# Window attention and a feed-forward block in float32: from three split products to one plain product, on one Trainium2 core

## The chip, the cores and the metric

The kernel runs on one core of one Trainium2 chip. The metric is the device time of one execution in microseconds (us). A core has a matrix engine (TensorE: PE for its matrix multiplications, PEld for the loads of the stationary operand), a vector engine (DVE), an activation engine (ACT), GpSimd (POOL) and a queue that issues DMA transfers (SP). Each of them works through its own list of instructions in order; semaphores make one wait for another.

## The reference, cut to what matters

Attention over 8 batches and 8 heads: 512 local positions with a window of 32 to either side, 32 global positions, 64 features a head. Its output, one row of 512 features for every position, is the input of a feed-forward block with 2048 hidden features.

```python
k_all = np.concatenate([k_g, k_l], axis=2); v_all = np.concatenate([v_g, v_l], axis=2)
out_g = np.matmul(sm(scale * np.matmul(q_g, k_all.transpose(0, 1, 3, 2))), v_all)
s_ll = np.where(mask, scale * np.matmul(q_l, k_l.transpose(0, 1, 3, 2)), -1000000000.0)
s_lg = scale * np.matmul(q_l, k_g.transpose(0, 1, 3, 2))
out_l = np.matmul(sm(np.concatenate([s_lg, s_ll], axis=-1)), v_all)
x = concatenate([out_g, out_l], axis=2)      # to (8*544, 512)
h = x @ w_in                                 # 512 -> 2048
return (h - np.tanh(h)) @ w_out              # 2048 -> 512
```

The attention inputs are float32; the two weights arrive in a 64-bit format and are turned into float32 on the chip.

## The kernel before, in words

**The work.** All matrix products run on TensorE, into eight PSUM banks of 128 x 512 float32. There are two kinds of operand: plain float32 (`F32`) and the rounded type `F32R`. Where a product has `F32R` operands, each operand x is held as a high part (x rounded to `F32R`) and a low part (x minus the high part), and the product is the sum of three: high x high, high x low and low x high.

**Feed-forward** (class `Chunk`). One chunk is 512 rows (the 512 local positions of a batch) or, at the end, the 256 global rows of all batches. It has 16 steps (8 for the 256 rows), one for each 128 hidden features. In a step `add_hidden` issues three groups of four products of 128 x 128 by 128 x 512 (line 1054: high weights by high x, high weights by low x, low weights by high x), ACT takes the tanh (line 1062), DVE subtracts (line 1065), a copy rounds the result to `ghi` (line 1068) and POOL or DVE subtracts to get `glo` (line 1071). `add_out` issues three groups of four products (line 1102: `w_out_hi` by `ghi`, `w_out_lo` by `ghi`, `w_out_hi` by `glo`), which add up in four banks over all 16 steps. After the last step the four banks are copied out and stored (lines 1125 and 1130).

**Attention.** Batches 0 and 1 (class `Pair`, and `Head` with `plain`) work in plain float32, two heads together: keys and queries are turned by TensorE (line 479), the scores of the global queries are two products a pair (lines 512 and 513), the local scores four a head (line 766), the softmax is on DVE, ACT and POOL, the probabilities are turned by TensorE (lines 552 and 858), and eight products a head with the values follow (line 956). Batches 2 to 7 (class `Head`) work one head at a time with split operands: keys and queries are turned by DVE and split, DMA transfers put the parts one under the other, so that one product of 128 rows holds two of the three (lines 712, 713, 769, 770); the values and the probabilities are split too (line 956), and the turning of the next head's probabilities is put between the products (line 958).

**Weights.** `add_weights` loads each weight in 64 pieces of 128 x 256 (256 KB as they arrive), joins the two 32-bit words (lines 375, 379, 383) and splits the result into `w_in_hi`, `w_in_lo`, `w_out_hi`, `w_out_lo` (lines 386 and 389). The pieces are spread over batches 0 and 1.

**What sets the order.** No engine's order is written out. Class `Order` is a planner: every operation is added with the engines it may run on, a planned duration, a due time, what it reads and writes and the PSUM banks it takes. `run` places them one by one at the earliest start, ties going to the earlier due time, and the instructions are issued in that order. Due times come from a table of numbers (`CFG`). The feed-forward of batch b is placed among the attention of batch b + 1, so TensorE's list alternates between the two; batch 0's attention has no feed-forward beside it, and the last batch's feed-forward and the global rows have no attention beside them.

Of the kernel before, what the change touches and what calls it, by code (L numbers as in the profile page):

```python
# [9 lines left out]
F32R = mybir.dt.float32r  # L10
# [11 lines left out]


def f32(ap):
    return ap.bitcast(F32)
# [7 lines left out]
class Later:  # L33


    def __init__(self, pool, shape, tag):
        self.make = lambda: pool.tile(shape, F32R, name=tag, tag=tag)
        self.tile = None

    def __call__(self):  # L40
        if self.tile is None:
            self.tile = self.make()
        return self.tile


class Op:
    __slots__ = ("eng", "fn", "due", "n", "ready", "succ", "alloc", "free", "lat", "start", "end", "args", "seq", "xfer", "rows", "ldw", "tail", "lock")


class Order:  # L50
# [14 lines left out]
    def add(self, eng, fn, due, r=(), w=(), res=(), alloc=(), free=(), lat=0.0, xfer=0.0, rows=1.0, ldw=0.107, tail=0.107, lock=False):  # L65
# [5 lines left out]
        o.xfer, o.rows, o.ldw, o.tail = xfer, rows, ldw, tail  # L71
# [22 lines left out]

    def tensor_time(self, t, d, rows):
        t0 = t
        while d > 1e-9:
            i = int(t / self.TICK + 1e-9)
            rate = 1.0 if self.columns.get(i - 1, 0) >= 3060 else 0.5
            x = min(d / rate, (i + 1) * self.TICK - t)  # L100
            self.columns[i] = self.columns.get(i, 0) + x * rate * 2400 * rows
            d -= x * rate
            t += x
        return t - t0

    def run(self):
# [3 lines left out]
        tail = 0.0  # L110
# [5 lines left out]
        while left:  # L116
            best = None
            for o in ready:
# [13 lines left out]
                for e, (d, pen) in o.eng.items():  # L132
# [3 lines left out]
                    if e == "T":  # L136
                        s = max(s, at.get(e, 0.0) + self.XW * max(0.0, o.ldw - tail))
# [9 lines left out]
            if e == "T":  # L147
                s = max(at.get(e, 0.0) + max(0.0, o.ldw - tail), ready_at)
                d = self.tensor_time(s, d, o.rows)
                tail = o.tail  # L150
# [31 lines left out]
def kernel(ctx, tc, q_l, k_l, v_l, q_g, k_g, v_g, w_in, w_out, out):  # L182
# [7 lines left out]
    NF = DFF // P  # L190
    WIDE = w_in.dtype != F32
# [4 lines left out]

    NPG = 4 * P + 96
    pg = cp.tile([P, NPG], F32, name="pg")
    idr = cp.tile([P, P], F32R, name="idr")
    idn = f32(idr)  # L200
    masks = [cp.tile([P, KC], BF16, name=f"mask{j}") for j in range(3)]
    tile_mask = [masks[0]] + [masks[1]] * (NT - 2) + [masks[2]]


    rawkq = cp.tile([P, 2 * S], F32, name="rawkq")
    raw1, kq = rawkq[:, :S], rawkq[:, S:]
    wraw = [cp.tile([P, 256, 2], F32, name=f"wraw{j}") for j in range(3)]
    tt_ = [cp.tile([P, 512], F32, name=f"t{j}") for j in range(2)]
    gg = [[cp.tile([P, 512], F32R, name=f"g{n}{j}") for n in ("hi", "lo")] for j in range(2)]
    stats = [cp.tile([P, 16], F32, name=f"st{j}") for j in range(3)]  # L210
    gt = cp.tile([P, 5, G], F32, name="gt")
    qgt = cp.tile([P, H, 2, G], F32R, name="qgt")


    prob = [cp.tile([P, 2 * KC + G], F32, name=f"prob{j}") for j in range(2)]
    prob = [prob[t // 2][:, t % 2 * KC:t % 2 * KC + 256] for t in range(NT)]
    prob2 = [t.rearrange("p (a c) -> p a c", a=2)[:, j] for t in tt_ for j in range(2)]
    vraw = cp.tile([P, 2, NT, D], F32, name="vraw")

    w_in_hi = cp.tile([P, NCC, DFF], F32R, name="w_in_hi")  # L220
    w_in_lo = cp.tile([P, NCC, DFF], F32R, name="w_in_lo")
    w_out_hi = cp.tile([P, NF, DM], F32R, name="w_out_hi")
    w_out_lo = cp.tile([P, NF - 4, DM], F32R, name="w_out_lo")
    xg = cp.tile([P, NCC, B * G], F32, name="xg")

    first_raw = cp.tile([P, 2, 2, NT, 2, D], F32, name="first_raw", tag="x_hi1")  # L230
    first_raw = [first_raw[:, 0], first_raw[:, 1], rawkq.rearrange("p (a t h d) -> p a t h d", a=2, t=NT, h=2)]
    first_kw = cp.tile([P, 2, 2 * S], F32, name="first_kw", tag="x_lo1")
    first_kw = [first_kw[:, 0, :NT * KC], first_kw[:, 1, :NT * KC], cp.tile([P, NT * KC], F32, name="first_kw2", tag="kw")]
    first_kw = [x.rearrange("p (t c) -> p t c", t=NT) for x in first_kw]
    first_q = cp.tile([P, 4 * DM], F32, name="first_q", tag="w_out_lo4")
    first_q = [first_q[:, :S], first_q[:, S:2 * S], cp.tile([P, S], F32, name="first_q2", tag="hi0")]
    first_q = [x.rearrange("p (t c) -> p t c", t=NT) for x in first_q]
    first_m = cp.tile([P, 2 * S], F32, name="first_m", tag="hl")
    first_mask = first_m[:, :608]
    first_t = cp.tile([P, 2, 2, 320], F32, name="first_t0", tag="thi"), cp.tile([P, 2, 2, 320], F32, name="first_t1", tag="tlo")  # L240
    first_v = cp.tile([P, 2, NT, 2, D], F32, name="first_v", tag="vv")
    first_g = cp.tile([P, H // 2, G], F32, name="first_g", tag="kgt")

    first_gq = first_m[:, 608:608 + H * G].rearrange("p (j h g) -> p j h g", j=H // 2, h=2)
    SETS = [[f"{n}{u}" for n in ("rk", "rq", "pw", "pk", "pq")] for u in range(2)] + [["raw", "kq", "kw0", "kg0", "hk0"]]


    kw2 = Later(cp, [P, NT, KC], "kw")
    hi0, hl = Later(cp, [P, S], "hi0"), Later(cp, [P, 2, S], "hl")

    def parts_hi(u):
        return hl()[:, 0] if u else hi0()

    def part_lo():
        return hl()[:, 1]

    x_hi = [cp.tile([P, NCC, S], F32R, name="x_hi0"), Later(cp, [P, NCC, S], "x_hi1")]
    x_lo = [cp.tile([P, NCC, S], F32R, name="x_lo0"), Later(cp, [P, NCC, S], "x_lo1")]
    w_out_lo4 = Later(cp, [P, 4, DM], "w_out_lo4")

    thi, tlo = [Later(cp, [P, 2, 2, 320], n) for n in ("thi", "tlo")]
    vv = Later(cp, [P, 2, NT, 2, D], "vv")
    kgt = Later(cp, [P, H * G], "kgt")

    def activations(b):
        return [t[0] if b % 2 == 0 else t[1]() for t in (x_hi, x_lo)]

    def low_out(f):
        return w_out_lo[:, f] if f < NF - 4 else w_out_lo4()[:, f - (NF - 4)]
# [4 lines left out]
    def bank(shape, j, dt=F32):  # L274
# [3 lines left out]
        t = banks[j][:shape[0], :n].bitcast(dt)  # L278
# [7 lines left out]
    CFG = dict(a_g=0.162, a_gl=0.0755, a_kg=0.0172, a_kq=0.0, a_ph=0.0, a_qs=0.8185, a_v=0.2532, a_w=0.0, a_wn=0.5965,  # L286
               a_xg=1.5017, d_g=0.0247, d_gl=0.1975, d_kg=6.9442, d_kq=6.391, d_ph=2.9141, d_pl=0.1314, d_qh=2, d_qs=1.1145,
               d_tg=0.3627, d_tp=2.2867, d_v=5.3766, d_w=2.1966, d_wl=1.4574, d_wn=0.0, d_xg=1.0089, d_y=1.8311, gfirst=0,
# [28 lines left out]
    def subtract(n, kind):  # L317
        return [("P", (0.17 + n * 0.00218), 0.0), ("D", (n + 151) / 960, CFG.get("s_" + kind, PENP), True)]
# [5 lines left out]
    def base(i):  # L324
        if i < H:
            return i * P0
# [1028 lines left out]
```

## Time and profile before

| | before |
|---|---|
| median of 3 runs | 1065.21 us (1061.15 to 1073.21) |
| the profiled execution's own time | 1064.42 us |
| its span, first to last instruction | 1062.5 us |
| mean granted TensorE clock | 0.989 of full speed |
| busy: PE, PEld | 1029.6 us, 863.3 us |
| busy: DVE, ACT, POOL | 665.7 us, 616.1 us, 625.1 us |
| moved by DMA | 91.70 MB |

Busy time counts each engine by itself. The products on TensorE are pipelined: the profile gives one a start and a duration that reaches into the next, so what one costs in a row of them is read from start to start and not from its duration. A row such as `128*64 128x512` gives the stationary operand (rows*columns) and the moving one (rows x columns). A row of the timeline merges neighbours: start, length of the whole run, engine, line, and how many records (x4). "The chain" is the work that ended last, followed back from the last instruction to whatever released each step.

### The profile page before, as it was taken

The numbers are of one execution on the slowest core, as the hardware profiler recorded it, in microseconds if no ns is written. First come the engines' busy times: TensorE is split into PE (matmuls) and PEld (weight loads), VectorE is DVE, ScalarE is ACT, GpSimd is POOL, SyncE is SP. The second block draws the span as 40 slices with busy tenths as digits, with TensorE's granted clock in tenths as the row PEclk, the third lists the DMA queues.
The fourth block names the chain that finished last, engine by engine and source line by source line (L and its number), as shares of the span: only waits on it lengthen the run. The fifth ranks groups of instructions, "written<-read, shape, count | busy, mean of one in ns | idle before, by whom it ended". The sixth has DMA issues, their size and how long they took to land.

```text
span 1062.5 us, 19221 instructions
## 1 busy us (share of the span) xinstructions
PE 1029.6 (97%) x5656; PEld 863.3 (81%) x5656; DVE 665.7 (63%) x2112; ACT 616.1 (58%) x1704; POOL 625.1 (59%) x875
## 2 busy tenths in 40 slices
PE   6989999999998999999999999999999999999998
PEld 4777777788887888888888888888887888888896
DVE  7865654566876786577766886577757776322221
ACT  6856656566766775487647766577647765311121
POOL 5544545556776776677756776577666766522211
PEclk9988999999999999999999999999999999999999
DMA  8553433453435443354335442453325331000010
GB/s 200 152 137 94 126 109 95 100 127 69 89 76 116 103 87 72 77 134 89 74 68 132 92 86 60 94 129 85 80 59 133 86 75 42 30 10 1 1 40 20
DMA packets 253640, 91.70 MB, mean 86 GB/s; under 512 B 205408, under 2 KB 238944, under 8 KB 253536
## 3 DMA queue, kind: packets, MB, share of 16 engines
q1 hardware_dynamic: 253536, 90.48, 36.1%
q8 instruction: 45, 0.74, 0.3%
q14 instruction: 59, 0.48, 0.2%
HBM read 49.27 MB, written 8.91 MB: 55 GB/s over the span
## 4 chain that ended last, share of the span: by engine, by line
PE 92%; DVE 3%; DMA 2%; SPq 1%; issue 1%; POOL 1%; ACT 1%; DVEq 0%; ACTq 0%; POOLq 0%
PE bank L1102 35%; PE bank L1054 35%; PE bank L956 8%; PE bank L958 4%; PE bank L769 2%; PE bank L766 2%; PE bank L770 2%; PE bank L858 1%; PE bank L712 1%; DMA wraw<-in_moe_w_in_dram 1%; PE bank L512 1%; PE bank L713 0%; SPq L893 0%; DMA wraw<-in_moe_w_out_dram 0%; DVE wraw L383 0%
## 5 line engine op out<-in xcount | busy, mean ns | idle before, releaser
L1071 POOL TENSOR_TENSOR glo<-t,ghi 128x512 fp32r<-128x512 f32 x136 | 175.6, 1292 | 190.7 <-DVE ghi L308 87.2
L1065 DVE TENSOR_TENSOR t<-bank,t 128x512 f32<-128x512 f32 x136 | 93.8, 690 | 175.6 <-ACT t L1062 173.6
L1062 ACT ACTIVATE t<-bank 128x512 f32<-128x512 f32 x136 | 81.4, 599 | 201.9 <-PE bank L1054 181.3
L1102 PE MATMUL bank<-w_out_lo,ghi 128*128 128x512 f32 x544 | 154.9, 399 | 0.0
L1102 PE MATMUL bank<-w_out_hi,ghi 128*128 128x512 f32 x544 | 154.4, 398 | 0.0
L794 POOL TENSOR_SCALAR prob<-prob,st 128x224 f32<-128x224 f32 x240 | 108.6, 465 | 76.6 <-DVE st L789 51.1
L1102 PE MATMUL bank<-w_out_hi,glo 128*128 128x512 f32 x544 | 152.9, 395 | 0.0
L1054 PE MATMUL bank<-x_lo,w_in_hi 128*128 128x512 f32 x512 | 142.5, 400 | 0.0
L1054 PE MATMUL bank<-x_hi,w_in_hi 128*128 128x512 f32 x512 | 141.6, 399 | 0.0
L1054 PE MATMUL bank<-x_hi,w_in_lo 128*128 128x512 f32 x512 | 140.4, 396 | 0.0
L781 ACT ACTIVATE prob<-prob,st 128x224 f32<-128x224 f32 x240 | 113.3, 474 | 17.4 <-DVE st L774 16.0
L1102 PEld LDWEIGHTS bank<-w_out_hi,ghi 128*128 128x128 f32 x544 | 101.0, 189 | 21.6 <-issue 0.5
L1102 PEld LDWEIGHTS bank<-w_out_hi,glo 128*128 128x128 f32 x544 | 99.4, 188 | 20.5 <-issue 0.6
L774 DVE CUSTOM_DVE_ANT_0 prob<-bank,mask 128x224 f32<-128x224 f32 x240 | 83.5, 388 | 51.4 <-PE bank L770 35.2
L1102 PEld LDWEIGHTS bank<-w_out_lo,ghi 128*128 128x128 f32 x544 | 99.3, 189 | 18.7 <-issue 0.3
L1054 PEld LDWEIGHTS bank<-x_hi,w_in_hi 128*128 128x128 f32 x512 | 94.7, 190 | 20.1 <-ACT x_hi L308 0.3
L1054 PEld LDWEIGHTS bank<-x_hi,w_in_lo 128*128 128x128 f32 x512 | 92.7, 189 | 18.2 <-issue 0.6
L1054 PEld LDWEIGHTS bank<-x_lo,w_in_hi 128*128 128x128 f32 x512 | 92.1, 191 | 16.6 <-issue 0.3
L958 PE MATMUL bank<-idr,prob 128*128 128x128 f32 x376 | 98.1, 281 | 1.5 <-POOL prob L794 1.0
L993 POOL TENSOR_TENSOR x_lo<-wraw,x_hi 64x256 fp32r<-64x256 f32 x96 | 70.8, 737 | 43.9 <-ACT x_hi L308 30.3
L956 PE MATMUL bank<-thi,vv 128*128 128x160 f32 (+2 forms) x384 | 96.4, 293 | 0.0
L956 PE MATMUL bank<-tlo,vv 128*64 128x160 f32 (+2 forms) x384 | 89.3, 233 | 0.0
(136 smaller groups left out, 1992.0 us busy)
## 6 DMA issues: line engine op xcount, KB each, us to landing
hl<-hl SPq DMA_DIRECT2D x72, 128.0 KB, 2.3
wraw<-in_moe_w_in_dram SPq DMA_DIRECT2D x32, 256.0 KB, 2.9
wraw<-in_moe_w_out_dram SPq DMA_DIRECT2D x32, 256.0 KB, 2.9
out_dram<-wraw SPq DMA_DIRECT2D x32, 256.0 KB, 2.3
kw<-hl SPq DMA_DIRECT2D x72, 96.0 KB, 2.2
vraw<-in_v_l_dram SPq DMA_DIRECT2D x48, 128.0 KB, 2.2
rawkq<-in_k_l_dram SPq DMA_DIRECT2D x96, 64.0 KB, 2.3
rawkq<-in_q_l_dram SPq DMA_DIRECT2D x96, 64.0 KB, 2.3
```

The source lines that it names most:

```text
L766: nc.tensor.matmul(t_[:, i, :KC], self.q[r, t], self.kw[r, t], start=True, stop=True)
L774: nc.vector.tensor_tensor_reduce(out=self.prob[t][:, :KC], in0=getattr(self, f"s_{pair}")[:, i, :KC], in1=tile_mask[t], scale=-0.125, scal ...
L781: nc.scalar.activation(x, x, AF.Exp, bias=self.st[:, t:t + 1], scale=-1.0, accum_out=self.st[:, 4 + t:5 + t])
L794: nc.gpsimd.tensor_scalar(x, x, self.st[:, 8 + t:9 + t], 1.0, op0=ALU.mult, op1=ALU.mult)
L956: nc.tensor.matmul(dst, l, r, start=i == 0, stop=i == len(mm) - 1, skip_group_check=True)
L958: nc.tensor.transpose(*turns[i // each], idn)
L993: eng[e].tensor_sub(places()[1], view(total, [(160, 2), (1, P)]), f32(places()[0]))
L1054: nc.tensor.matmul(self.h[s][:, j * n:(j + 1) * n], w[:, cc, f * P:(f + 1) * P], self.x()[xi][:, cc, :n], start=part == 0 and cc == 0 and ...
L1062: nc.scalar.activation(tt_[q], self.h[s], AF.Tanh)
L1065: nc.vector.tensor_sub(tt_[q], self.h.pop(s), tt_[q])
L1071: eng[e].tensor_sub(gg[q][1], tt_[q], f32(gg[q][0]))
L1102: nc.tensor.matmul(self.acc[tt], g[:, j * self.n + tt * P:j * self.n + (tt + 1) * P], low_out(f) if wi else w_out_hi[:, f], start=s == 0 a ...
```

## The change

All splitting goes. Every product of the feed-forward and of the attention of every batch has plain float32 operands and is issued once: a feed-forward step is four products in `add_hidden` and four in `add_out`, with no `ghi`, `glo`, `x_lo` or low weights. The attention of batches 2 to 7 takes the form that batches 0 and 1 had (`Pair`), so the splits, DVE's turning and the DMA transfers between tiles go. In the freed memory the tiles get more copies: three hidden tiles in place of two, three sets of keys and queries, three of probabilities, four of turned probabilities, two of values. The global scores of a pair use four heads' queries side by side (128 stationary columns in place of 64). Weights come in 32 pieces of 128 x 512 (512 KB), and the join writes straight into the weight tile. The planner's table is new, with a planned 0.43 for each product of 512 columns and a planned price for changes of the operand's shape (`FORM`).

```diff
-            for part in range(3):
-                wi, xi = ((0, 0), (0, 1), (1, 0))[part]
-                r = [k + (xi,) for k in self.xkeys] + [("w", "i", f, j, wi) for f in fs for j in range(2)]
-                add(("T", 0.92), mm(part), due + 0.1 * part, r=r, w=[hk],
-                    res=[tk] if part == 0 else (), alloc=[(hk, "h")] if part == 0 else ())
+            add(("T", 4 * 0.43), mm, due, r=self.xkeys + [("w", "i", f) for f in fs], w=[hk], res=[tk], alloc=[(hk, "h")])
...
-            add(either(512, "g"), high, due + 2, r=[tk], w=[gk])
-            add(subtract(512, "g"), rest, due + 2, r=[tk, gk], w=[lk])
...
-            passes = ((0, 0), (1, 0), (0, 1))
...
-                        nc.tensor.matmul(self.acc[tt], g[:, j * self.n + tt * P:j * self.n + (tt + 1) * P],
-                                         low_out(f) if wi else w_out_hi[:, f], start=s == 0 and k == 1, stop=last and k == 3 * self.per)
+                        nc.tensor.matmul(self.acc[tt], tt_[q][:, j * self.n + tt * P:j * self.n + (tt + 1) * P], w_o[:, f],
+                                         start=f == 0, stop=f == NF - 1)
...
+                        nc.tensor.matmul(self.h[s][:, j * n:(j + 1) * n], w_i[:, cc, f * P:(f + 1) * P], self.x[:, cc, :n],
+                                         start=cc == 0 and j == 0, stop=cc == NCC - 1 and j == self.per - 1,
...
-    pieces = [(kind, f, j) for f in range(NF) for kind in "io" for j in range(2)]
+    pieces = [(kind, f) for f in range(NF) for kind in "io"]
...
+    w_i = cp.tile([P, NCC, DFF], F32, name="w_i")
+    w_o = cp.tile([P, NF, DM], F32, name="w_o")
+    xx = tiles(2, [P, NCC, S], "x")
...
+NRAW, NKW, NV, NPROB, NTURN, NHID = 2, 3, 2, 3, 4, 3
...
+    pairs = [Pair(j) for j in range(B * HP)]
+
+    def attention(j):
+        p = pairs[j]
+        p.add_turn()
+        p.add_scores()
...
+        for a in p.heads:
+            a.add_scores()
+        p.add_transpose()
+        for a in p.heads:
+            a.add_transpose(0)
+            a.add_transpose(1)
+            a.add_products()
```

On TensorE's list, in the middle of the program, where a feed-forward chunk stands among another batch's attention, the rows before read as follows. A row gives the line, the operation, what it writes and reads (`x_hi`, `x_lo` the split input, `w_in_hi` and its like the split weights, `kw` and `hl` the split keys and queries), the size of the product and how many stand together.

```order
L1054 MATMUL bank_104<-x_hi_1079,w_in_hi 128x512 x4
L1102 MATMUL bank_107<-w_out_hi,glo_75 128x512
L1102 MATMUL bank_108<-w_out_hi,glo_75 128x512
L1102 MATMUL bank_105<-w_out_hi,glo_75 128x512
L1102 MATMUL bank_106<-w_out_hi,glo_75 128x512
L769 MATMUL bank_101<-kw,hl 128x224
L770 MATMUL bank_101<-kw,hi_1935 128x224
L769 MATMUL bank_101<-kw,hl 128x224
L770 MATMUL bank_101<-kw,hi_1935 128x224
L712 MATMUL bank_103<-kw,qgt 128x384
L713 MATMUL bank_102<-kw,qgt 128x224
L1054 MATMUL bank_104<-x_lo_1080,w_in_hi 128x512 x4
```

In the changed kernel the same part of TensorE's list reads so (`x` the input, `w_i` and `w_o` the weights, `t` the hidden tile, `kw` and `q` the turned keys and queries, `pg` the global probabilities):

```order
L648 MATMUL bank_108<-x_68,w_i 128x512 x4
L501 MATMUL bank_107<-kw_87,q_90 128x224 x2
L501 MATMUL bank_105<-kw_87,q_90 128x224 x2
L461 MATMUL bank_106<-idn,pg 128x64 x4
L461 MATMUL bank_106<-idn,pg 96x64
L680 MATMUL bank_111<-w_o,t_75 128x512
L680 MATMUL bank_109<-w_o,t_75 128x512
L680 MATMUL bank_112<-w_o,t_75 128x512
L680 MATMUL bank_110<-w_o,t_75 128x512
```

One hidden group (line 648) now fills a bank where three did, and one row of line 680 stands for each of the four accumulating banks where three did. The group of the next step (line 648) and some attention stand between a step's hidden group and its own rows of line 680.

At the end of batch 0's attention, where the first chunk begins, TensorE's list before has the last products with the values (line 956) and then the first groups of the feed-forward:

```order
L956 MATMUL bank_106<-first_t_96,first_v 128x160 x2
L956 MATMUL bank_106<-first_t_96,first_v 128x128
L956 MATMUL bank_106<-first_t_96,first_v 128x160
L1054 MATMUL bank_103<-x_hi_99,w_in_hi 128x512 x4
L1054 MATMUL bank_102<-x_hi_99,w_in_hi 128x512 x4
L1054 MATMUL bank_103<-x_lo_100,w_in_hi 128x512 x4
```

After the change the same place reads:

```order
L596 MATMUL bank_110<-turned_100,v_93 128x160
L341 MATMUL bank_106<-idn,graw 128x32 x8
L387 MATMUL bank_107<-idn,raw_83 128x128 x4
L387 MATMUL bank_105<-idn,raw_83 128x128 x4
L648 MATMUL bank_106<-x_68,w_i 128x512 x4
L648 MATMUL bank_108<-x_68,w_i 128x512 x4
```

The next batch's globals, keys and queries (lines 341 and 387) are turned ahead of the first hidden group, which was not so before.

More of the change, by code (lines that the diff above doesn't have):

```diff
@@ L238 @@
[L238 to L245, printed above, removed]
@@ L248 @@
[L248 to L261, printed above, removed]
@@ L262, with tiles @@
[L262 to L269, printed above, removed]
+    def tiles(n, shape, name, dt=F32):
+        return [cp.tile(shape, dt, name=f"{name}{j}") for j in range(n)]
+    idn = cp.tile([P, P], F32, name="idn")
+    masks = tiles(3, [P, KC], "mask", BF16)
+    tile_mask = [masks[0]] + [masks[1]] * (NT - 2) + [masks[2]]
@@ L1318 @@
-    for c in chunks:
+    keys = [("xg", b * H + h, p) for b in range(B) for h in range(H) for p in range(2)]
+    last = Chunk(xg, keys, B * G, "g", global_rows, chunk.due + 400)
+    for c in (chunk, last):
         ffn_steps(c, 0, c.steps + 1)
```

975 lines of the change are left out of this document (290 added, 685 removed).

## The prediction, made before the changed kernel was timed

> **What bounds the kernel now.** I read the page first, then the chain in order of time, then TensorE's timeline where nothing else disturbs it. The page:
>
> ```profile
> span 1062.5 us, 19221 instructions
> PE 1029.6 (97%) x5656; PEld 863.3 (81%) x5656; DVE 665.7 (63%) x2112; ACT 616.1 (58%) x1704; POOL 625.1 (59%) x875
> PEclk9988999999999999999999999999999999999999
> PE 92%; DVE 3%; DMA 2%; SPq 1%; issue 1%; POOL 1%; ACT 1%; DVEq 0%; ACTq 0%; POOLq 0%
> ```
>
> TensorE is busy nearly throughout, the chain stands on it for 92% of the span, its clock is full but for the start, and no other engine passes 63%. So what takes load off DVE, ACT, POOL and DMA is worth nothing by itself, and the question is only how long TensorE's own list becomes. The chain in order of time shows the beat: each batch's feed-forward closes with the same run of rows.
>
> ```profile
> 447.48 2.76 PE bank L1102 x12
> 563.76 2.76 PE bank L1102 x12
> 680.01 2.76 PE bank L1102 x12
> 796.74 2.76 PE bank L1102 x12
> ```
>
> From one to the next it is 116.3, 116.3 and 116.7 us: a stage of one batch's feed-forward and the next one's attention takes 116.4 us. The price of a rounded product stands at the end, where the feed-forward is alone:
>
> ```profile
> 1000.41 1.08 PE L1102 MATMUL bank<-w_out_hi,glo 128*128 128x512 f32 x4
> 1001.33 1.08 PE L1054 MATMUL bank<-x_hi,w_in_hi 128*128 128x512 f32 x4
> 1002.25 1.08 PE L1102 MATMUL bank<-w_out_hi,ghi 128*128 128x512 f32 x4
> ```
>
> From start to start it is 0.92 us for four, so 0.23 each. A batch has 64 products in line 1054 and 64 in line 1102, each made three times: 128 x 3 x 0.23 = 88.3 us of the 116.4. The attention of a batch with split operands takes the other 28.1.
>
> **What a plain product costs.** The change trades three rounded products for one plain one, so this price decides everything, and the trace has it, because batches 0 and 1 work in plain float32 already.
>
> ```profile
> 184.26 0.54 PE L766 MATMUL bank<-first_kw,first_q 64*128 64x224 f32 x2
> 184.73 1.07 PE L512 MATMUL bank<-first_kw,first_m 128*64 128x512 f32 x2
> 185.64 0.33 PE L513 MATMUL bank<-first_kw,first_m 128*64 128x96 f32 x2
> 185.90 1.19 PE L1054 MATMUL bank<-x_lo,w_in_hi 128*128 128x512 f32 x4
> ...
> L512 PE MATMUL bank<-first_kw,first_m x16: 592/643/1114, 8.6 to 185.2; 128*64 128x512 f32 x16
> L766 PE MATMUL bank<-first_kw,first_q x128: 349/349/577, 10.9 to 199.9; 64*128 64x224 f32 x128
> ```
>
> Line 512 is executed once a pair, eight times in all, and has 16 records: a plain product is two records. In the run of two at 184.73 the last lasts 0.59, so it began at 185.21, and the next operation began at 185.64, 0.43 later. One record of 512 columns holds TensorE for 0.43 us, almost twice the 0.23 of a whole rounded product, and a plain product needs two: 0.86 us against 3 x 0.23 = 0.69. The smaller form says the same: two records of line 766 last 0.54, the last one 0.35, so 0.19 apart at 224 columns, and 0.19 x 512/224 = 0.43. Line 766 too has 128 records for 16 heads x 4 products. The stationary operand of line 512 has only 64 columns; the feed-forward's has 128. For that form there is line 956:
>
> ```profile
> 59.44 1.16 PE L956 MATMUL bank<-first_t,first_v 128*128 128x160 f32 x8
> 60.44 0.60 PE L858 MATMUL bank<-idr,prob 128*128 128x128 f32 x4
> 60.87 1.21 PE L956 MATMUL bank<-first_t,first_v 128*128 128x160 f32 x8
> 61.92 0.60 PE L858 MATMUL bank<-idr,t 128*128 128x128 f32 x4
> 62.45 0.51 PE L552 MATMUL bank<-idr,pg 64*128 64x64 f32 x5
> 62.89 0.66 PE L858 MATMUL bank<-idr,t 128*128 128x128 f32 x4
> ```
>
> Eight records are four products of 160, 160, 128 and 128 columns (1.00 us to the next start) or of 160, 160, 128 and 160 (1.05 us): 1.00 x 512/576 = 0.89 and 1.05 x 512/608 = 0.88 for 512 columns. That is the upper bound, since the narrow products carry more fixed time each. The lower bound for a record is the 0.23 of a rounded product, so 0.46 for two; nothing in these rows comes near it. I take 0.858 (0.429 a record), from line 512, whose moving side has the feed-forward's width.
>
> The Trainium skill, in its page FP8 and Floating Point Precision, section TensorE Precision Notes, has true float32 as four passes through the array. Counted as four times the 0.23 row that would be 0.92 a product and 67 us more over the program; two records of 0.43 are less, so by the trace the passes are cheaper here than four rounded products.
>
> **The change part by part.** *Feed-forward.* 8 batches x 128 products of 512 columns, and for the global rows 64 products of 256 columns (32 of 512) and 32 of 512: 1088 in all. Before 1088 x 0.69 = 750.7, now 1088 x 0.858 = 933.5: plus 183 us, all on TensorE.
>
> *Attention of batches 2 to 7.* A pair of heads in the plain form, from the rows above: local scores 2 heads x (8 records x 0.19 + 0.1 for the change of shape) = 3.24; products with the values 2 x (1.00 + 1.05) = 4.10; turned probabilities four groups of four at 0.43 (60.44 to 60.87) = 1.72; keys and queries, two such groups, 0.86; global scores 0.91 + 0.26 (184.73 to 185.64 to 185.90) = 1.17; turned global probabilities 0.44 (62.45 to 62.89). That is 11.5 a pair and 46.1 a batch, against 28.1 now: plus 18.0, and over six batches plus 108 us. Batches 0 and 1 keep their form; their global scores go to 128 stationary columns, which by line 956 costs nothing.
>
> *What goes elsewhere.* The splits (lines 1068, 1071, 389, 993), DVE's turning and the transfers between tiles disappear. They run beside a TensorE that never waits long for them, so I cost them at nothing. What is left on DVE and ACT a stage (softmax, tanh, subtraction, copies) is less than now, and the stage is longer.
>
> ```profile
> 333.00:449.00 116.00, 112.52 (x635) 95.74 (x634) 82.15 (x250) 74.96 (x210) 78.92 (x112) 0.99 0.41 90
> 449.00:565.00 116.00, 114.61 (x657) 97.84 (x656) 83.55 (x257) 76.64 (x213) 80.51 (x113) 1.00 0.41 92
> ```
>
> In this table by stretches (length, then PE, PEld, DVE, ACT and POOL busy) DVE works 82 to 84 of 116 us; if none of it left it would still fit into 160. PE is idle for 1.4 to 3.5 us of a stage; I allow 3.
>
> *The start.* Before, the first hidden group begins at 73.8, while DVE is the fullest engine beside the chain:
>
> ```profile
> L1054 PE MATMUL bank<-x_hi,w_in_hi x512: 387/393/655, 73.8 to 1002.0; 128*128 128x512 f32 x171
> 0.00:27.00 27.00, 18.32 (x99) 12.35 (x100) 20.79 (x95) 16.91 (x53) 13.86 (x35) 1.00 0.83 200
> 27.00:53.00 26.00, 24.30 (x155) 19.35 (x153) 23.25 (x96) 21.47 (x70) 15.27 (x26) 1.00 0.54 152
> ```
>
> Batch 0's attention is 46 us of TensorE work in both kernels. The changed list puts only a few weight loads into this stretch and has no splits in it, so DVE and ACT have less there; but the softmax still has to be waited for. Between 48 (work alone, and a first load) and 74 (as now) I take 60: minus 14. On SP's queue a weight load now waits for one of four buffers until DVE has joined the piece before, and the loads of values and keys for the next pair stand behind it; TensorE has 0.86 x 8 = 6.9 us of work for each pair of pieces, so a late piece would cost a few us in the first stage only.
>
> *The end.*
>
> ```profile
> 1056.94 0.40 PE L1102 MATMUL bank<-w_out_hi,glo 128*128 128x512 f32 x1
> 1057.41 0.59 ACT L308 COPY wraw<-bank 128x512 f32<-128x512 f32 x1 [0.79 <-PE bank L1102]
> ```
>
> The last product ends at 1057.3, and 5.2 us of copy and store follow, as now.
>
> *The sum.* Against the span: 1062.5 + 183 + 108 - 14 = 1339.5. By stages: 60 to the first hidden group; seven stages of 128 x 0.858 + 46.1 + 3 = 158.9, so 1112; the last batch's feed-forward 109.8 and the global rows 64 x 0.858 = 54.9; the end 5.2: 1342. I take a span of 1343. The profiled execution took 1064.42 for its 1062.5, so 1345 us, and the median of the runs (1065.21) is not 1 us from that execution.
>
> **The rivals.** *A record streams like a rounded product (faster).* The planner's table in the diff has 0.43 for a whole product, which would be two records of 0.215; rows of the profile have 0.43 for one. If records of 128 x 128 by 512 went at the 0.23 of the rounded ones, the feed-forward would be 1088 x 0.46 = 500 us, a pair about 7.6 (scores, products and global scores halved), a stage 58.9 + 30.4 + 3 = 92, and the whole 52 + 646 + 88 + 5 = 791, or about 795 us. It decides the sign below 0.33 us a record: (1343 - 1062)/(1343 - 791) = 0.51 of the way from 0.43 to 0.23. Against it stand all three plain forms, that with 128 x 128 stationary included.
>
> *A plain product costs four rounded ones (slower still).* Then 0.92 for 512 columns: 1088 x 0.062 = 67 more, 1412 us. The records at 0.43 speak against it; that the wide form with 128 stationary columns is not in the trace speaks for it, and the 0.88 and 0.89 of line 956 lie between.
>
> *TensorE waits in every step (slower still).* With one group where there were three, the tanh and the subtraction (lines 1062 and 1065) have less work to hide behind. If each of 136 steps waited for both, 0.6 + 0.7 us by their rows,
>
> ```profile
> L1065 DVE TENSOR_TENSOR t<-bank,t 128x512 f32<-128x512 f32 x136 | 93.8, 690 | 175.6 <-ACT t L1062 173.6
> L1062 ACT ACTIVATE t<-bank 128x512 f32<-128x512 f32 x136 | 81.4, 599 | 201.9 <-PE bank L1054 181.3
> ```
>
> that is 136 x 1.3 = 177 more, 1520 us. Against it: the next step's hidden group, 4 x 0.858 = 3.4 us, stands between in TensorE's list, and there are three hidden tiles.
>
> **How the numbers follow.** The forecast has a chance of 0.85, the first rival 0.05, the second 0.05, the third 0.04, and 0.01 is for an end near the time before. The forecast's own unknowns: the record by line 956 instead of line 512 (1088 x 0.03 = 33 up), the start (12 down, 14 up), the idle time (3 us a stage, all seven away or doubled: 21). Added as independent that is 1345 less some 25 and plus some 40; because one mis-read row moves all 1088 products at once I widen it to 1300 to 1400. A measurement tells apart about 1% (11 us). Faster by more than that: 0.05; within: 0.01; slower: 0.94.
>
> **What would show it right or wrong.** In the profile after, lines 648 and 680 should have two records a product (1152 and 1088), 0.43 apart from start to start and some 0.6 long; the chain should stand on TensorE for over 92%, with some 70% on those two lines; the beat of a stage should be 159 us; the first record of line 648 should come near 60; DVE, ACT and POOL should fall to under half of the span. One record a product, or records 0.2 apart, would make the first rival true and the forecast wrong; idle time ahead of line 680 that ACT or DVE ends would make the third.

## The result and the profile after

The changed kernel takes 1328.58 us (median of 4 runs, 1328.04 to 1329.48) against 1065.9 us for the kernel before in the same comparison (median of 4 runs, 1061.15 to 1073.21): 1.2458 times as long, with a 95% interval of 1.2386 to 1.253. The change makes the kernel slower by a quarter. The forecast was 1345 us within 1300 to 1400; it is 16 us too high.

The page of the changed kernel shows the span, the busy time of each engine, the granted clock, the chain by engine and by line, and the two costliest groups:

```profile
span 1326.3 us, 14383 instructions
PE 1316.1 (99%) x4896; PEld 747.5 (56%) x4896; DVE 383.5 (29%) x1470; ACT 401.9 (30%) x1150; POOL 142.0 (11%) x305
PEclk9999999999999999999999999999999999999999
PE 99%; DVE 0%; DMA 0%; SPq 0%; issue 0%; POOL 0%; POOLq 0%; DVEq 0%
PE bank L648 36%; PE bank L680 36%; PE bank L596 10%; PE bank L501 8%; PE bank L545 4%; PE bank L387 2%; PE bank L421 2%; PE bank L461 1%; PE bank L422 0%; PE bank L341 0%; DMA raw<-in_q_l_dram 0%; SPq L373 0%; DVE pg L426 0%; SPq L333 0%; POOL pg L438 0%
L680 PE MATMUL bank<-w_o,t 128*128 128x512 f32 x1088 | 494.4, 595 | 0.0
L648 PE MATMUL bank<-x,w_i 128*128 128x512 f32 x1024 | 462.5, 595 | 0.0
```

Everything but TensorE became much lighter: DVE falls from 665.7 to 383.5 us, ACT from 616.1 to 401.9, POOL from 625.1 to 142.0. None of that shortens anything, because the chain stands on TensorE for 99% and TensorE's own list became 286.5 us longer (1029.6 to 1316.1 us busy). That is more than the whole loss of 263.8 us; the difference is idle time that TensorE had before and has no more (32.9 us outside records before, 10.2 after). It issues fewer matmul records, 4896 in place of 5656, but most of them are of the dearer kind. Its only waits of any size in the whole span are these (line, what it waited for: us in total, times, the longest):

```profile
PE bank L341 <- DVE bank L747: 3.5, 1, 3.5
PE bank L461 <- POOL pg L438: 1.1, 1, 1.1
PE bank L387 <- DMA raw<-in_q_l_dram: 0.3, 1, 0.3
```

The chain in order of time shows the new beat of a stage and the price of a record. Where it stays with one line, a row has the length of an unbroken run of that line:

```profile
59.48 6.89 PE bank L648 x16
...
374.12 7.06 PE bank L648 x16
...
531.04 7.06 PE bank L648 x16
...
687.95 7.06 PE bank L648 x16
...
844.86 7.06 PE bank L648 x16
...
1159.76 6.87 PE bank L648 x16
...
1276.53 6.91 PE bank L648 x32
1310.98 10.31 PE bank L680 x24
```

A stage takes 156.9 us (374.12 to 531.04, and the next two the same to 0.01), where it took 116.4. In the last row 24 records take 10.31 us, 0.430 each. A product is two of them, 0.86 us, in place of three rounded ones at 0.23. The row of 32 has records of 256 columns at 0.216 each, so the time goes with the columns. That the records are two a product is counted in the lists of the two lines: the hidden product has 1024 records of 512 columns and 128 of 256 for the 512 + 64 products that the code issues, and line 680 has 1088 for 544 (records x; duration in ns min/median/max; first and last start; the form behind the semicolon is counted on a sample where there are many records).

```profile
L648 PE MATMUL bank<-x,w_i x1024: 590/592/697, 59.3 to 1255.3; 128*128 128x512 f32 x171
L648 PE MATMUL bank<-xg,w_i x128: 379/379/379, 1262.6 to 1310.6; 128*128 128x256 f32 x128
```

The stage by engines, in the table by stretches, has TensorE without a gap and DVE, ACT and POOL at 42, 47 and 17 of 157 us:

```profile
374.00:531.00 157.00, 157.00 (x592) 88.23 (x590) 42.27 (x173) 47.49 (x139) 17.03 (x36) 1.00 0.14 33
531.00:688.00 157.00, 157.00 (x590) 88.27 (x590) 42.26 (x173) 47.50 (x140) 17.00 (x36) 1.00 0.14 33
```

### The profile page after: what moved, and what is told of

Its sections match the earlier page's. It is cut to its first block, busy times and chain, and to the rows that moved or that the text cites. A ratio compares the mean times of both kernels' runs of the same rounds, so it can differ in the third digit from the quotient of the medians.

```text
span 1326.3 us, 14383 instructions
## 1 busy us (share of the span) xinstructions
PE 1316.1 (99%) x4896; PEld 747.5 (56%) x4896; DVE 383.5 (29%) x1470; ACT 401.9 (30%) x1150; POOL 142.0 (11%) x305
## 4 chain that ended last, share of the span: by engine, by line
PE 99%; DVE 0%; DMA 0%; SPq 0%; issue 0%; POOL 0%; POOLq 0%; DVEq 0%
PE bank L648 36%; PE bank L680 36%; PE bank L596 10%; PE bank L501 8%; PE bank L545 4%; PE bank L387 2%; PE bank L421 2%; PE bank L461 1%; PE bank L422 0%; PE bank L341 0%; DMA raw<-in_q_l_dram 0%; SPq L373 0%; DVE pg L426 0%; SPq L333 0%; POOL pg L438 0%
## 5 line engine op out<-in xcount | busy, mean ns | idle before, releaser
L680 PE MATMUL bank<-w_o,t 128*128 128x512 f32 x1088 | 494.4, 595 | 0.0
L648 PE MATMUL bank<-x,w_i 128*128 128x512 f32 x1024 | 462.5, 595 | 0.0
L680 PEld LDWEIGHTS bank<-w_o,t 128*128 128x128 f32 x1088 | 197.2, 190 | 204.0 <-issue 203.6
L648 PEld LDWEIGHTS bank<-x,w_i 128*128 128x128 f32 x1024 | 187.1, 190 | 202.0 <-issue 200.9
L596 PEld LDWEIGHTS bank<-turned,v 128*128 128x128 f32 (+1 forms) x1024 | 135.8, 190 | 24.3 <-issue 23.8
L247 ACT COPY turned<-bank 128x512 f32<-128x512 f32 (+2 forms) x222 | 85.6, 429 | 200.1 <-PE bank L545 146.9
L596 PE MATMUL bank<-turned,v 128*128 128x160 f32 (+2 forms) x1024 | 140.3, 290 | 0.1
L501 PEld LDWEIGHTS bank<-kw,q 64*128 64x128 f32 x512 | 90.1, 186 | 40.4 <-issue 34.4
L501 PE MATMUL bank<-kw,q 64*128 64x224 f32 x512 | 112.8, 362 | 0.0
L545 PE MATMUL bank<-idn,prob 128*128 128x128 f32 (+1 forms) x512 | 74.5, 274 | 0.0
```

What stands on the lines that cost most here:

```text
L247: (nc.scalar.copy if e == "A" else nc.vector.tensor_copy)(dst, src)
L501: nc.tensor.matmul(self.s[t // 2][:, t % 2, :KC], q[r, t], kw[r, t], start=True, stop=True)
L545: nc.tensor.transpose(t[:n, a, i], self.prob[:, 2 * pair + i, a * P:a * P + n], idn)
L596: nc.tensor.matmul(t_[:, o0:o0 + c1 - c0], self.v[:k, a, t].rearrange("p h d -> p (h d)"), self.turned[:k, pair, a, c0:c1], start=i == 0, ...
L648: nc.tensor.matmul(self.h[s][:, j * n:(j + 1) * n], w_i[:, cc, f * P:(f + 1) * P], self.x[:, cc, :n], start=cc == 0 and j == 0, stop=cc == ...
L680: nc.tensor.matmul(self.acc[tt], tt_[q][:, j * self.n + tt * P:j * self.n + (tt + 1) * P], w_o[:, f], start=f == 0, stop=f == NF - 1)
```

## The experiments

The theory is that of the forecast: TensorE bounds both kernels, and the loss is the price of a plain product, two records of 0.43 us, against three rounded ones of 0.23. The main rival says that the loss, or a good part of it, comes from somewhere else in the change: the hidden tile on its way through ACT and DVE, the attention's new form, the new weights, the order. Runs without an interval are single executions beside one of the kernel before on the same chip, which then took between 1062.9 and 1064.8 us; they are compared with the changed kernel by the span of their profile, 1326.3 us. The spans of the changed kernel's four runs lie between 1326.3 and 1327.7 us, so differences of 9 us and more are well outside that scatter.

### The feed-forward's price alone: one rounded product

The weights, the input and the hidden tile get the rounded type; everything else stays as in the changed kernel.

```diff
-    w_i = cp.tile([P, NCC, DFF], F32, name="w_i")
-    w_o = cp.tile([P, NF, DM], F32, name="w_o")
+    w_i = cp.tile([P, NCC, DFF], F32R, name="w_i")
+    w_o = cp.tile([P, NF, DM], F32R, name="w_o")
...
-        add(("D", 0.69), join, due, r=[key, key + ("up",)], w=[wk], lock=True)
+        add(("D", 0.69), join, due, r=[key + ("up",)], w=[key], lock=True)
+        add([("D", 0.43, 0.0, True), ("A", 0.62, 0.0)], rounded, due, r=[key], w=[wk])
```

> The changed kernel with the feed-forward's operands in the rounded type, each product made once (the low parts are left out; the attention stays plain; 32 weight pieces get one more copy, which rounds them). Theory, the type's price on TensorE is all: 1088 products of 512 columns go from 0.858 to 0.23 us, 683 us less than 1326, so about 645 us, up to 720 if the shorter steps let TensorE wait for tanh and subtraction. Rival, the order or the waits set the time and not the type: above 1200 us.

It took 666.24 us, with a span of 664.4: the loss turns into half the time by the type of the feed-forward's operands alone. On its page TensorE is no longer the whole chain, and the products with the weights have one record each (544 for 544):

```profile
PE 85%; ACT 4%; DVE 4%; DMA 3%; issue 1%; POOL 1%; SPq 0%; DVEq 0%; ACTq 0%; POOLq 0%
...
L686 PE MATMUL bank<-w_o,t 128*128 128x512 f32 x544 | 161.7, 414 | 0.5 <-DVE t L662 0.4
```

So neither the hidden tile's way nor the attention holds the changed kernel at its time; they fit into half of it. The time is some 20 us over the 645 that this run's sum gave; about half of that is time outside records, 20.2 us here (664.4 less 644.3 busy) and 10.2 in the changed kernel; the other half was not followed.

### Three rounded products, without the splitting

As the run before, but each rounded product is issued three times. The high product is thus added up three times over; the low parts and the work that makes them are left out.

```diff
-                    for cc in range(NCC):
+                    for k in range(3 * NCC):
+                        cc = k % NCC
...
+                        for k in range(3):
+                            nc.tensor.matmul(self.acc[tt], tt_[q][:, j * self.n + tt * P:j * self.n + (tt + 1) * P], w_o[:, f],
+                                             start=f == 0 and k == 0, stop=f == NF - 1 and k == 2)
```

> As ffn_once, but each rounded product is made three times in a row (the high product thrice in place of high and low parts; no splitting work). Theory: 1088 x 3 x 0.23 = 751 in place of 933 us, so 183 less than 1326: 1143 us, and the 80 us that are left above the kernel before are the plain attention's. Rival, the feed-forward's type costs nothing and the attention makes the whole loss: 1326 us, no change. Rival, the feed-forward makes the whole loss: 1065 us.

It took 1154.34 us, with a span of 1152.5. This kernel has the feed-forward's TensorE work of the kernel before and the attention of the kernel after, so it cuts the loss of 263.8 us in two: 90.0 us lie between the kernel before and this one (attention and start, forecast 108 - 14 = 94), and 173.8 between this one and the kernel after (the feed-forward, forecast 183). The cut is good to a few us only, because the planner put TensorE's list into a somewhat different order here. By the two counts that are explained two sections on (165 changes of shape and 37 starts side by side here, 153 and 49 in the changed kernel) that is an estimated 12 x 0.09 + 12 x 0.19 = 3 us. Its page has the forecast's kinds of rows, three records where the change has two:

```profile
PE 97%; DVE 1%; ACT 0%; POOL 0%; DMA 0%; issue 0%; SPq 0%; POOLq 0%; DVEq 0%
...
L687 PE MATMUL bank<-w_o,t 128*128 128x512 f32 x1632 | 410.5, 399 | 0.0
```

### The scores' price alone

Keys and queries get the rounded type, so that local and global scores are one rounded product each in all eight batches. The feed-forward stays plain.

```diff
-    kws = tiles(NKW, [P, NT, KC], "kw")
-    qs = tiles(NKW, [P, NT, P], "q")
+    kws = tiles(NKW, [P, NT, KC], "kw", F32R)
+    qs = tiles(NKW, [P, NT, P], "q", F32R)
```

> The changed kernel with the attention's keys and queries in the rounded type, so that local and global scores are one rounded product each (their low parts are left out). Theory: a local score product goes from 2 x 0.19 to 0.11 us, eight a pair, and the global ones from 1.05 to 0.34 a pair: 2.9 x 32 = 92 us less, 1234 us. Rival, the attention hides beside the feed-forward and only the feed-forward counts: 1326 us.

It took 1245.51 us, with a span of 1243.7, 82.6 us less where 92 were expected. The rule that two plain records become one cheaper one holds in the attention too. The missing 9 us were not followed.

### Does the work beside TensorE matter?

The changed kernel gets back, in every step, a copy on ACT and a subtraction on POOL of the size that splitting the hidden tile had. What they write is not used.

```diff
+    junk = tiles(2, [P, 512], "junk")
...
+            def again(e, _):
+                nc.scalar.copy(junk[0], tt_[q])
+
+            def rest(e, _):
+                nc.gpsimd.tensor_sub(junk[1], tt_[q], junk[0])
+
+            add(("A", 0.62), again, due + 2, r=[tk], w=["junk0"])
+            add(("P", 1.29), rest, due + 2, r=[tk, "junk0"], w=["junk1"])
```

> The changed kernel with the copy and the subtraction of a split put back in every feed-forward step (a copy of the hidden tile on ACT, 0.6 us, and a subtraction on GpSimd, 1.3 us, 136 of each), into a tile that nobody reads. Theory, the splits ran beside TensorE and their removal was worth nothing: no change, 1320 to 1340 us. Rival, they were on the path: up to 136 x 1.9 = 258 us more, 1585 us.

It took 1347.08 us, with a span of 1345.3: 19 us more, where the theory expected none. The theory missed. Its page shows where they went:

```profile
PE 1332.1 (99%) x4896; PEld 756.9 (56%) x4896; DVE 404.6 (30%) x1513; ACT 467.1 (35%) x1243; POOL 315.9 (23%) x441
```

The longest of TensorE's waits in that kernel do not make 19 us:

```profile
PE bank L342 <- DVE bank L757: 3.5, 1, 3.5
PE bank L388 <- ACT q L248: 1.2, 5, 0.2
PE bank L462 <- POOL pg L439: 1.1, 1, 1.1
PE bank L546 <- ACT turned L248: 0.7, 1, 0.7
```

Instead TensorE is busy for 16 us more with the same 4896 records. Because the planner knows of the added work, it puts TensorE's list into another order. Two things that depend on the order can be counted in the trace from start to start. A change between operands of 64 or 32 rows (lines 501, 461 and 341) and wider ones adds some 0.09 us (429 ns become 523, 189 become 280), while one between 96 and 128 rows adds nothing (136 ns stay 136): the changed kernel has 153 such changes, this one 197 (the expectation below counts one more). And two 64-row records in different halves of the rows can start almost together: the changed kernel has 49 such starts less than 40 ns after another, this one 5. An estimate from these counts, with 0.19 for a record of line 501 that is hidden, is 44 x 0.09 + 44 x 0.19 = 12.3 us of the 19. Another 3 us are longer waits: TensorE is outside records for 13.2 us here and for 10.2 in the changed kernel. The rest was not followed. To tell the order from the work, the same work was put behind the tanh and the subtraction inside their own operations, so that the planner does not see it and TensorE's list stays the changed kernel's, row for row:

```diff
+                nc.scalar.copy(junk[0], tt_[q])
+                nc.gpsimd.tensor_sub(junk[1], tt_[q], junk[0])
```

> The split's copy (ACT) and subtraction (GpSimd) back in every step as in split_work_back, but issued right behind the hidden tile's subtraction without the planner knowing, so that TensorE's list is the changed kernel's row by row. Theory after split_work_back: its 19 us came from another order on TensorE (198 changes of the operand's row shape against 153, 5 starts side by side against 49), not from the work itself; with the same order 1322 to 1332 us. Rival, the work itself delays TensorE: 1340 to 1347 us again.

It took 1327.97 us, with a span of 1326.2, the changed kernel's to 0.1 us:

```profile
PE 1316.0 (99%) x4896; PEld 747.4 (56%) x4896; DVE 393.4 (30%) x1470; ACT 478.1 (36%) x1286; POOL 314.7 (24%) x441
```

ACT carries 76 us and POOL 173 us more than in the changed kernel, and the end does not move. This settles the step "I cost them at nothing" for the hidden tile's splits: that load beside TensorE costs nothing here, and the 19 us came with the other order.

### Two hidden tiles in place of three

```diff
-NRAW, NKW, NV, NPROB, NTURN, NHID = 2, 3, 2, 3, 4, 3
+NRAW, NKW, NV, NPROB, NTURN, NHID = 2, 3, 2, 3, 4, 2
```

> The changed kernel with two hidden tiles in the ring in place of three. Theory, one hidden group of 3.4 us covers tanh and subtraction of 1.3 us, so the third tile is not needed: no change, 1320 to 1340 us. Rival, TensorE would wait for them in every step without it: up to 136 x 1.3 = 177 us more, 1500 us.

It took 1337.93 us, with a span of 1335.9. That is inside the expected range, but it is 9.6 us more and not "no change"; the beat is 158.5 us. Its list of waits is that of the changed kernel with one row of 0.4 us more, but its order has 177 changes of shape and 13 starts side by side, which by the same prices makes 24 x 0.09 + 36 x 0.19 = 9.0 us. A first try to part the tile from the order kept the changed kernel's order and put the sums into two tiles. In that order some products with `w_out` stand behind the tanh of the step two on, so with two tiles they take that later step's hidden values: part of the computation is changed, and TensorE waits for values that it did not need.

> Two hidden tiles in the ring as in two_hidden_tiles, but planned with three, so that TensorE's list is the changed kernel's row by row. Theory: the 10 us of two_hidden_tiles came from the order (177 changes of row shape against 153, 13 starts side by side against 49): 24 x 0.09 + 36 x 0.19 = 9 us, so with the same order 1322 to 1332 us. Rival, TensorE waits for the tile: 1336 us or more.

It took 1350.53 us with a span of 1348.7, outside the expected range, and for the reason given it does not decide the question. The other way round does: the order planned for two tiles, with the sums written to three tiles in turn.

```diff
-    tt_ = tiles(NHID, [P, 512], "t")
+    tt_ = tiles(NHID + 1, [P, 512], "t")
...
+            z = (step_no[0] - 1) % 3
```

> The order of every engine is planned as for two hidden tiles, but the sums are written to three tiles in turn, so the tile of a step is never one that the step before last could still be reading. The kernel with two tiles had a span of 1335.9 us, the changed kernel with three 1326.3. If order alone makes the difference: 1335.9, within 1 us. If the lack of a third tile makes TensorE or ACT wait: the waits go and the span is some 9 us shorter, near 1326.

It took 1337.39 us, with a span of 1335.3. The third tile in the same order gives back 0.6 us of 9.6. The rows of its chain in order of time have the beat of 158.5 us that the kernel with two tiles has:

```profile
375.31 7.07 PE bank L649 x16
533.80 7.06 PE bank L649 x16
692.29 7.06 PE bank L649 x16
```

So TensorE does not wait for hidden tiles, with three or with two; what the third tile changes is the order that the planner finds.

### The halves of the array side by side

The local scores of a pair's two heads, one in rows 0 to 63 and one in rows 64 to 127, are issued in turn: for every tile of 128 queries first one head and then the other, in one operation for both.

```diff
+                    for t in (2 * pair, 2 * pair + 1):
+                        for a in self.heads:
+                            r = slice(a.e, a.e + D)
+                            nc.tensor.matmul(a.s[pair][:, t % 2, :KC], q[r, t], kw[r, t], start=True, stop=True)
```

> The changed kernel with the local scores of a pair's two heads put alternately (head 0 in rows 0 to 63, head 1 in rows 64 to 127 of the stationary side) instead of one head after the other. Theory of the prediction, each record holds TensorE for its whole time: no change, 1320 to 1340 us. Rival, records in different halves of the rows run side by side, as 6 ns from a start of the scores to a start of the turned global probabilities in the changed kernel's trace suggests: half of 16 x 0.19 a pair goes, 1.5 x 32 = 48 us, about 1278 us.

It took 1317.44 us, with a span of 1315.6: 10.7 us less. The busy times on its page:

```profile
PE 1291.3 (98%) x4896; PEld 712.5 (54%) x4896; DVE 379.3 (29%) x1469; ACT 402.3 (31%) x1151; POOL 144.1 (11%) x305
```

The costlier ones of TensorE's waits in that kernel:

```profile
PE bank L341 <- DVE bank L772: 3.5, 1, 3.5
PE bank L387 <- DVE st L538: 3.3, 5, 0.8
PE bank L570 <- POOL prob L553: 2.3, 4, 0.8
PE bank L341 <- DVE q L247: 1.5, 4, 0.4
PE bank L570 <- DVE st L547: 1.3, 2, 1.0
```

TensorE is busy for 24.8 us less (1316.1 to 1291.3) with as many records: 239 starts now lie less than 40 ns behind another, where there were 49. So the halves do work at the same time. But its time outside records grew from 10.2 us to 24.3. TensorE now waits a little in many places, most of all for the softmax on DVE and POOL. A likely reason, not shown, is that the joint operation needs two banks at once. Its list also has 187 changes of shape in place of 153, an estimated 3 us at 0.09 each, which are part of the busy time. Neither theory is right: the gain exists, but the span fell by 10.7 us and not by 48, and more than half of what TensorE's busy time lost came back as waits.

### Everything rounded, once

The feed-forward and the attention's scores and products with the values, all in the rounded type with one product each. All low parts are left out, so this computes less than either kernel, and it shows what is left when TensorE's price is taken away.

> The changed kernel with every product of the feed-forward and of the attention (scores and values) in the rounded type and made once: all low parts are left out. The theory's sum from the runs so far: 666 with the feed-forward rounded, less 81 for the scores (1326 to 1245 with these alone), less the values' products, 2.05 to some 1.0 a head, 64 us: 520 us if TensorE still sets the time, up to 590 if tanh, softmax and the copies on ACT (408 of 664 us busy with the feed-forward rounded) become what it waits for. Rival, the gains do not add since ACT already bounds: 640 to 666 us.

It took 580.17 us (median of 4 runs, 574.83 to 581.34), 0.5439 of the kernel before (0.5413 to 0.5465), the fastest of all that ran. The mean granted clock of the profiled execution was 0.957 here. The chain is at last shared:

```profile
PE 54%; DVE 17%; ACT 15%; issue 6%; DMA 5%; POOL 1%; DVEq 0%; ACTq 0%; SPq 0%; POOLq 0%
```

### The start

In the kernel before, the weight loads were given due times 64 us later, with no other number changed (the planner then places every operation anew), to see whether they delay the first hidden group there.

```diff
-               s_v=0.0096, s_w=1.5188, s_wl=6.2098, step=14.8192, step1=24.0941, lag0=9.8205, hs0=6.7392, tol=0.0448, wd0=-43.8484,
+               s_v=0.0096, s_w=1.5188, s_wl=6.2098, step=14.8192, step1=24.0941, lag0=9.8205, hs0=6.7392, tol=0.0448, wd0=20.0,
```

> The kernel before with one number of its table changed, so that the weight pieces are loaded and split later (their due time 64 us later). In the changed kernel the first hidden group comes at 59.3 us, in the one before at 73.8; theory: that is because the weights' joining and splitting stood among batch 0's softmax, so with later weights the first group comes some 5 to 14 us sooner and the time falls by as much, 1051 to 1060 us. Rival, batch 0's softmax alone sets the start, or the later weights hold up the first chunk: no change or up to 20 us more.

It took 1086.95 us (median of 5 runs, 1082.05 to 1090.83), 1.0206 times the kernel before (1.0182 to 1.023). The theory missed. The first hidden group came at 70.2 in place of 73.8, a quarter of the 14.5 us that the changed kernel gained, and the first stage paid for it: between 80 and 106 TensorE is busy for 21.60 us at a granted clock of 0.70, where the kernel before has 25.06 at 0.87. The row of the table by stretches with the late weights:

```profile
80.00:106.00 26.00, 21.60 (x69) 15.57 (x69) 12.10 (x38) 11.15 (x31) 9.73 (x13) 0.70 0.28 86
```

The same stretch of the kernel before:

```profile
80.00:106.00 26.00, 25.06 (x115) 18.94 (x116) 14.31 (x57) 16.59 (x48) 12.21 (x19) 0.87 0.31 93
```

So moving the weight loads gave back a quarter of the start at most. The run is a partial test: of the 64 pieces (32 of each weight), 12 were still joined in the first 60 us, where the kernel before joined 18 and the changed kernel 5 of twice the size. The traces show another piece of the start. TensorE's last wait ahead of the first hidden group stands in front of the products with the values of batch 0's last pair (line 956): 3.57 us before, ending at 67.12, and 4.24 with late weights, ending at 63.95. The profile names ACT's work on a weight piece as what ended it. But these products also wait for the values of the pair's second head. Their first piece was issued at 63.89 and landed at 66.87 before, and was issued at 60.66 and landed at 63.71 with late weights, so the products could have begun at most 0.25 us sooner. The kernel before has one tile for a pair's values, which the pair ahead has to let go first; the changed kernel has two. No run gives the kernel before a second one, so how much of the 14.5 us this is stays open, as does the share of the splits in the two-batch start, of the banks of three hidden groups a step and of the order, which are all gone together in the changed kernel.

## Why the prediction was right

**The bound.** That TensorE sets the end of the changed kernel is shown from both sides: 249 us of added work on ACT and POOL cost nothing in the same order, and changing the type of the feed-forward's operands alone halves the time. For the kernel before it rests on its chain, 92% on TensorE, and on the run of three rounded products without the splitting, which lies 90.0 us above it where the forecast put 94 on attention and start; no run takes load off the other engines of the kernel before itself.

**The price.** 0.858 us for a plain product of 512 columns, read from two records of line 512 with 64 stationary columns, held for 128 stationary columns: 24 records in 10.31 us are 0.859 a product. The upper bound from line 956 (0.88 to 0.89) was too high, as the forecast argued: the form of 160 columns measures 0.136 a record from start to start in the changed kernel, 0.435 scaled to 512, that of 128 columns 0.109 to 0.113, 0.436 to 0.452 scaled, and that of 512 itself 0.429.

**The parts.** The cut by three rounded products puts 174 us on the feed-forward (forecast 183) and 90 on attention and start (forecast 94). The first hidden group came at 59.3, forecast 60. A stage took 156.9, forecast 158.9. DVE, ACT and POOL fell to 29%, 30% and 11%, forecast under half. Lines 648 and 680 carry 72% of the chain, forecast some 70%.

**Where the 16 us are.** They are two errors of opposite sign, so it is partly luck that the sum is this close. The term that was mis-sized is idle time: 14 us in the start beyond its 46 of work, 3 us in each of seven stages and 5.2 at the end made 40 us, while the profile after shows 10.2 us outside records in the whole span. The allowance of 3 us a stage had been carried over from a kernel in which DVE was busy for 82 to 84 of 116 us, into one in which it is busy for 42 of 157 and TensorE for all of them. The other way, TensorE's own work was set too low: 933.5 for the feed-forward and 8 x 46.1 for the attention make 1302 us, and 1316.1 were busy. The stage shows it in small: 156.9 - 109.8 = 47.1 us of attention, 1 more than forecast. The forecast had two changes of shape a pair (64) and the list has 153; an estimate of 89 x 0.09 = 8 us over the eight batches would be that 1 us, but the 49 starts side by side work the other way, so this part of the account is rough.

**The rivals.** Records that stream like rounded ones fell by the record counts and 0.43 us. Four rounded products fell by 0.859 against 0.92; the sum by four times the rounded row would have been 83 us too high. The Trainium skill (FP8 and Floating Point Precision, TensorE Precision Notes) has true float32 as four passes; the trace shows two records a product and cannot tell passes, so it does not speak against four (0.859 / 4 = 0.215 each), only against pricing a pass at the 0.23 of a rounded product. Waits in every step fell by the list of waits: no row of line 680 is in it.

**Not foreseen** was that the order of the same records is worth 9 to 19 us on this engine. The forecast had treated TensorE's list as a sum of prices, which do not depend on what stands next to what.

## What to carry to other kernels

When one engine carries the chain, price a change of number format on that engine first: count the records that one product of each format makes, and read a record's price from start to start in a form that the kernel already has. In this kernel relief for the other engines was worth nothing while TensorE carried the chain, and an idle allowance should not be carried from a loaded stage into one that the change empties. If a kernel differs from another in a small way and a planner is allowed to react, run it once more in the kept order before the difference is blamed on the edit.

## What the runs showed of the hardware

A plain float32 product is two records, and each takes 0.84 to 0.85 ns a column from start to start (429 ns for 512, 216 for 256, 136 for 160, 109 for 128; medians of the trace), whether the stationary operand has 64 or 128 columns. Rounded products of 512 columns take 0.23 us in one record.

Two plain records of 64 rows in different halves of the rows run side by side. The timeline of TensorE in the changed kernel shows a piece of it; line 501 works in one half here and line 461 in the other:

```profile
234.45 1.21 PE L501 MATMUL bank<-kw,q 64*128 64x224 f32 x5
235.32 0.40 PE L461 MATMUL bank<-idn,pg 64*128 64x64 f32 x3
235.50 0.35 PE L501 MATMUL bank<-kw,q 64*128 64x224 f32 x1
235.55 0.28 PE L461 MATMUL bank<-idn,pg 64*128 64x64 f32 x2
```

The fifth record of the first row starts at 235.310 and the first of the second row at 235.317, 7 ns later, while records of line 501 among themselves are 0.19 us apart. The Trainium skill (TensorE: Matmul & The Clock Gate, Part 3: Packing small matmuls, The mechanism) says that tiles in different rows overlap with starts some 4 ns apart; the trace agrees that they overlap, for plain float32, with the 49 starts of the changed kernel 6 to 10 ns apart. The change between 64 or fewer rows and more costs about 0.09 us each time (429 ns become 523, 189 become 280).
